# First block of a fused SSM and SwiGLU kernel: a row sent by another engine, one tile's statistics on another engine, an earlier copy, and buffers at other addresses

## The chip, the cores and the metric

The kernel runs on one core of a Trainium2 chip. The metric is the device time of one execution in microseconds (us). A core has five engines that run their own instruction queues in order and wait for one another by semaphores: TensorE (PE; its weight loads are shown apart as PEld), VectorE (DVE), ScalarE (ACT), GpSimd (POOL) and SyncE (SP). SyncE and ScalarE issue the DMAs of this kernel.

## The reference

2048 tokens of 448 channels pass through two branches, each with a layer norm that a small conditioning vector shifts, scales and gates.

```python
x = A_u
mod = (_silu(c) @ w_mod).reshape(c.shape[0], 6, 1, -1)
sa, ca, ga, sb, cb, gb = (mod[:, 0], mod[:, 1], mod[:, 2], mod[:, 3], mod[:, 4], mod[:, 5])
h = _layernorm(x, axis=-1) * (1 + ca) + sa
x = x + ga * _A_ref(h, ...)      # state-space convolution along the tokens
h = _layernorm(x, axis=-1) * (1 + cb) + sb
x = x + gb * _B_ref(h, ...)      # (silu(h @ w_gate) * (h @ w_up)) @ w_down, 1792 hidden
```

## The kernel before

**Tiles and blocks.** A tile is 128 tokens by 448 channels. The sixteen tiles form six blocks of 2, 2, 3, 3, 3 and 3. A prologue computes the modulation rows, a test flag and the first branch of tiles 0 and 1. Then `run_blocks` goes block by block: `ffn` does the second branch of the block, and between its matmuls the first branch of the next block's tiles is done.

**Slices.** In `ffn` the hidden width is cut into 14 slices of 128. Slice f has `gate_up(f)` (L750: 22 matmuls with the tokens' high and low parts `hhi` and `hlo` as moving operand and the weights `gu` as stationary one), then ScalarE's SiLU (L765), VectorE's product (L778), and the product's high part `phi` (ScalarE, L785) and low part `plo` (VectorE, L786). `down(f)` (L798) multiplies these with the down weights' parts `wdh` and `wdl`, and stands one slice later on TensorE. In block 0 the weights are still raw: ScalarE makes the high parts (L122, L123, L115) and VectorE the low ones (L125, L117) in the course of the slices.

**The first branch.** For each tile of the next block: mean and variance, normalised and modulated h, then cumulative sums over tokens by matmuls with a triangular matrix (L978, L979 in block 0), to which a row carried from the tile before is added (`run0`, `run1`; added at L946 and L947 by VectorE). The carried row is computed on partitions 96 to 127 (L987, L988) and one small DMA takes partition 127's row to partition 0. Then the second norm's statistics follow, and at the end of the block `make_xn` (L207 to L209) and eight or twelve transposes (L220) give the next block's `hhi` and `hlo`.

**Order.** It is written by hand. In the prologue the string `PLAN` is the order; `qtb` is the copy of the gate row's four partial rows into `gb` (ScalarE), `gbk` the matmul that adds them up and spreads them (L495), `gb` its copy back, `xn0` the scaling of tile 0's normalised rows (L510). In the blocks `TIMES` gives half-slices: h places a step after `gate_up(h // 2)`, ahead of the down product (h even) or behind it (h odd). In block 0 statistics come from `Norm.sums`: ScalarE adds up a copy of the tile, GpSimd divides by 448, ScalarE adds up the squares of the differences. In later blocks `Norm.stat` takes them on VectorE with two instructions.

```python
                    at(0, 1, lambda: sc.dma_start(run[0:1], run[127:128]))
...
                    elif not b:
                        go(h, n2.sums, nx[q], nx, 0)
                        go(h + 1, n2.sums, nx[q], nx, 1)
```

Of the kernel before, what the change touches and what calls it, by code (L numbers as in the profile page):

```python
# [8 lines left out]
F32 = mybir.dt.float32  # L9
# [3 lines left out]
OP = mybir.AluOpType  # L13
# [16 lines left out]


TIMES = (
# [3 lines left out]
)  # L36
# [4 lines left out]
ORDER = """sf x0 x1 sc m10 se sd m11 m20 m21 m00 sb m01 sa m40 m41 m30 m31 w0 w1 d0 m50 m51 d1 x2 w2 x3 d2"""  # L41

PLAN = """t4 pa0 t1 S1 t2 pa1 t3 wi ca gp S20 wr ps0 h00 gpc gt h01 S21 psx gac a2 sq1 ps1 m0 dg gdm t5 k0 gdr S3 h10 cp v00 dga a3 o00
m1 k1 cpc gd h11 hd0 ck v01 sq0 o10 v10 w0 cbw o12 v11 w01 o01 o02 hd1 o13 o14 xh1 gc0 sa d00 gc1 st0 r0 sp x1 st1 r1 n10 gq fs spc n11 xn0 sbt qtb sbc fl l1
gbk tr0 xn1 xn1b gb tr1 hi00 hi01 hi10 tr1b lo00 lo01 hi11 lo10 lo11 w1 w11 fr1 fx"""
EPS = 1e-5

# [9 lines left out]
def tile_kernel(ctx, tc, x, a_re, a_im, b_re, b_im, c_re, c_im, log_dt,  # L57
# [78 lines left out]
    g0 = const.tile([128, D], F32)  # L136
    gm0 = const.tile([128, D], F32)
    gm1 = g0
    hhi = const.tile([128, 4, MB * 128], F32R)
    hlo = const.tile([128, 4, MB * 128], F32R)  # L140
    gd = const.tile([128, D], F32)
    sbc = const.tile([128, 4], F32)
    flag = const.tile([1, 1], I32)
    half = const.tile([128, 1], F32)

    small = ctx.enter_context(tc.tile_pool(name="small", bufs=2))

# [5 lines left out]
    class Norm:  # L153
# [10 lines left out]
        def sums(self, i, ts, z):  # L164

            if i == ts[0] and not z:
                self.mv = small.tile([128, MB, 2], F32, name="mv" + self.tag)
            m, v = (self.mv[:, i - ts[0], k:k + 1] for k in range(2))
            if not z:
                sc.activation(h_of(i), xs[i], AF.Copy, accum_out=m)  # L170
                po.tensor_scalar(m, m, 1.0 / D, None, op0=OP.mult)
            else:
                sc.activation(h_of(i), xs[i], AF.Square, scale=-1.0, bias=m, accum_out=v)

        def root(self, ts, summed=False):
            rs = small.tile([128, MB], F32, name="rs" + self.tag)
            n = len(ts)
            if summed:
                po.tensor_scalar(rs[:, 0:n], self.mv[:, 0:n, 1], 1.0 / D, EPS, op0=OP.mult, op1=OP.add)
            else:  # L180
                po.tensor_scalar(rs[:, 0:n], self.mv[:, 0:n, 1], EPS, None, op0=OP.add)  # L181
            po.tensor_tensor(rs[:, 0:n], rs[:, 0:n], mhalf.to_broadcast([128, n]), op=OP.pow)
            for q, i in enumerate(ts):
                self.of[i] = self.mv[:, q, 0:1], rs[:, q:q + 1]
# [30 lines left out]
    def transposes(ts):  # L215
        n = len(ts) * 128
        for k in range(4):
            ps = CV if k == 2 else bank()
            for j, i in enumerate(ts):
                pe.transpose(ps[:, j * 128:(j + 1) * 128], xn[i][:, k * 128:(k + 1) * 128], ident)  # L220
            parts(hhi[:, k, 0:n], hlo[:, k, 0:n], ps[:, 0:n], k)

    xd = [dram.tile([128, 512], F32, name=f"xd{q}") for q in range(MB)]

# [9 lines left out]
    def split_turned(ts):  # L234
        n, m = len(ts) * 128, len(ts)
        for k in range(4):
            hi, lo = (h[:, k, 0:n].rearrange("p (q a r) -> p q a r", q=m, a=4) for h in (hhi, hlo))
            parts(hi, lo, turned[:, 0:m, :, k, :], k)

    wp0 = ctx.enter_context(tc.tile_pool(name="wp0", bufs=1))  # L240
    ones = const.tile([128, 1], F32)
    mhalf = const.tile([128, 1], F32)
    ntok = const.tile([128, 1], F32)
    cs = const.tile([128, 5], F32)
    pick = const.tile([128, 1], F32)
    gac = const.tile([128, 4], F32)

    def mod_part(ps, w, ks):
# [34 lines left out]
    with tc.tile_pool(name="pre", bufs=1) as pre:  # L283
# [153 lines left out]

        def high(q, ks=range(4)):
            for k in ks:
                c_ = slice(q * 128, (q + 1) * 128)  # L440
                sc.activation(hhi[:, k, c_], pk[q, k][:, k * 128:(k + 1) * 128], AF.Identity, bias=sbc[:, k:k + 1])

        def high_v(q, ks):
            for k in ks:
                c_ = slice(q * 128, (q + 1) * 128)
                ve.tensor_scalar(hhi[:, k, c_], pk[q, k][:, k * 128:(k + 1) * 128], sbc[:, k:k + 1], None, op0=OP.add)

        def low(q, ks=range(4)):
            for k in ks:
                c_ = slice(q * 128, (q + 1) * 128)  # L450
                ve.scalar_tensor_tensor(hlo[:, k, c_], pk[q, k][:, k * 128:(k + 1) * 128], sbc[:, k:k + 1], f32(hhi[:, k, c_]),
                                        op0=OP.add, op1=OP.subtract)

# [272 lines left out]
    def run_blocks(pools, stages, first=None):  # L726
        work, hid = pools.work, pools.hid
        def ffn(ts, fresh, last, todo):
# [4 lines left out]
            def gate_up(f, nw):  # L733
                head = fresh and f < 2
                if fresh and f:
                    split_d(f)
                w = wgu[f]
                p = hid.tile([128, 256], F32, name="p") if fresh else p_of[f % 2]
                hi = hid.tile([128, MB * 128], F32R, name="phi")
                lo = hid.tile([128, MB * 128], F32R, name="plo")  # L740
                ps = [bank(), bank()]

                top = [(k, a) for k, ws in enumerate(((0, 6), (1, 5), (2, 4), (3,))) for a in ws]
                low = [(k, k) for k in range(4)]

                def mm(s, ka, lo, first=False, end=False):
                    for q, (k, a) in enumerate(ka):
                        pe.matmul(ps[s][:, 0:n], w[:, s, a], (hlo if lo else hhi)[:, k, 0:n],  # L750
                                  start=first and q == 0, stop=end and q == len(ka) - 1)
# [24 lines left out]
                if nw is not None:  # L776
                    split_w(nw, 0)
                ve.tensor_tensor(ps[1][:, 0:n], p[:, 0:n], ps[1][:, 0:n], op=OP.mult)  # L778
                if fresh and f == 0:
                    split_d(0, 1)  # L780
                    for g, a in todo.get("mid", []):
                        g(*a)
                elif nw is not None:
                    split_w(nw, 1)
                sc.copy(hi[:, 0:n], ps[1][:, 0:n])  # L785
                ve.tensor_tensor(lo[:, 0:n], ps[1][:, 0:n], f32(hi[:, 0:n]), op=OP.subtract)  # L786
                if fresh and f == 0:
                    split_w(nw, 1)
# [86 lines left out]
        for b, ts in enumerate(TILES):  # L875
            todo = {}
            if b + 1 < len(TILES):
# [14 lines left out]
                if b == 0 and first is None:  # L892
                    go(EXTRA[0], gate_0)
                    todo["mid"] = [(first_rows, ())]
                    at(0, 1, lambda: sc.dma_start(run[0:1], run[127:128]))
                for i, h in zip(nx, stat1):
                    if b:
                        go(h, n1.stat, i, nx)
                    else:
                        go(h, n1.sums, i, nx, 0)  # L900
                        go(h + 1, n1.sums, i, nx, 1)
                go(root1, n1.root, nx, not b)

                for h, q, z in sorted((h, q, z) for q, hs in enumerate(times) for z, h in enumerate(hs)):
                    if z < len(times[q]) - 1:
                        if z < len(st):
                            go(h, st[z], nx[q])
                    elif not b:
                        go(h, n2.sums, nx[q], nx, 0)
                        go(h + 1, n2.sums, nx[q], nx, 1)  # L910
                    elif late:
# [4 lines left out]
                        go(h + 1, make_xn, nx[q], t_of[q])  # L916
                        go(h + 2, turn, nx[q], q)
                if late:
                    go(late[0], n2.root, nx, not b)
# [5 lines left out]
    def small_path(pools):  # L925
# [58 lines left out]
        def s5(i):  # L984
            o, s = vs.pop(i)
            if i + 1 < NT:
                sc.copy(run1[end], s[end])  # L987
                ve.scalar_tensor_tensor(run0[end], run1[end], 128.0, o[end], op0=OP.mult, op1=OP.add)  # L988
                sc.dma_start(run[0:1], run[127:128])
            ve.tensor_tensor(xs[i], xs[i], o, op=OP.add)  # L990
            ve.scalar_tensor_tensor(xs[i], s, tok, xs[i], op0=OP.mult, op1=OP.add)

# [108 lines left out]
```

## Time and profile before

| | |
|---|---|
| median of 3 runs | 485.16 us (485.07 to 485.28) |
| the profiled execution | 485.64 us, of which 483.8 us from the first to the last instruction |
| TensorE matmul busy | 471.3 us, 97% |
| VectorE, ScalarE, GpSimd busy | 282.6 us (58%), 161.2 us (33%), 60.4 us (12%) |
| granted TensorE clock | 1.0 throughout |
| prologue, block 0, block 1, rest | 0 to 34.0, to 95.4, to 152.8, to 483.8 us |

Times of rows are counted from the span's start. Matmuls are pipelined, so the length of a matmul's row overlaps with the next one's; from one start to the next is what it takes. In brackets behind a row of the timeline stands how long the engine was idle ahead of it and what ended that.

### The profile page before, as it was taken

The page shows a single profiled execution, that of the slowest core. Times are in us where ns is not written, and L with a number is a line of the kernel's source. Part 1 is how long each engine was busy: PE and PEld are TensorE (multiplying, and loading weights), DVE is VectorE, ACT ScalarE, POOL GpSimd, SP SyncE. Part 2 cuts the span into 40 slices and gives each one's busy share as a digit, 9 for nine tenths or more (in the row PEclk, how much of TensorE's full clock was granted, in tenths as well). Part 3 has the DMA queues.
Part 4 walks back from the last instruction along what each step waited for, and adds up shares of the span by engine and source line. Part 5 has one row for each costly group of instructions (what it writes and reads, how often), then busy time and mean ns, then how long its engine had stood idle before and what let it go on. Part 6 is the DMA issues. An engine that isn't in the chain of part 4 may idle for free.

```text
span 483.8 us, 7024 instructions
## 1 busy us (share of the span) xinstructions
PE 471.3 (97%) x2735; PEld 445.5 (92%) x2735; DVE 282.6 (58%) x538; ACT 161.2 (33%) x363; POOL 60.4 (12%) x86
## 2 busy tenths in 40 slices
PE   6999999799999999999999999999999999999995
PEld 4659999699999999999999999999999999999995
DVE  5878997768785546573644756375475544221225
ACT  5868656522234222332312323221223232112111
POOL 1221000000000040310022320002241000000000
PEclk9999999999999999999999999999999999999999
DMA  8955653030001100111200011130001112000001
GB/s 307 416 212 170 195 181 103 0 96 2 1 2 46 51 1 0 45 41 48 95 20 1 2 44 45 43 115 0 2 0 45 45 43 77 22 2 0 1 0 63
DMA packets 18779, 31.24 MB, mean 65 GB/s; under 512 B 2608, under 2 KB 13488, under 8 KB 18736
## 3 DMA queue, kind: packets, MB, share of 16 engines
q1 hardware_dynamic: 18000, 30.52, 18.6%
q8 instruction: 23, 0.38, 0.4%
q10 hardware_dynamic: 736, 0.19, 0.2%
q14 instruction: 20, 0.16, 0.1%
HBM read 24.61 MB, written 6.03 MB: 63 GB/s over the span
## 4 chain that ended last, share of the span: by engine, by line
PE 86%; DVE 6%; ACT 3%; DMA 3%; issue 1%; SPq 0%; POOL 0%; ACTq 0%; DVEq 0%
PE bank L750 56%; PE dn L798 25%; DMA wm<-in_w_mod_groups_dram 2%; DVE gu L125 1%; DMA vec<-in_c_log_dt_dram 1%; DVE plo L786 1%; DVE wdl L117 1%; PE bank L252 1%; PE cv L968 1%; PE cv L966 1%; PE bank L967 1%; ACT gu L122 0%; DVE bank L778 0%; DVE x L837 0%; PE bank L220 0%
## 5 line engine op out<-in xcount | busy, mean ns | idle before, releaser
L750 PE MATMUL bank<-hhi,gu 128*128 128x384 f32 (+1 forms) x1176 | 213.0, 320 | 0.2 <-issue 0.2
L750 PEld LDWEIGHTS bank<-hhi,gu 128*128 128x128 f32 x1176 | 192.7, 188 | 3.5 <-issue 1.1
L750 PE MATMUL bank<-hlo,gu 128*128 128x384 f32 (+1 forms) x672 | 133.2, 320 | 0.0
L750 PEld LDWEIGHTS bank<-hlo,gu 128*128 128x128 f32 x672 | 111.0, 188 | 0.2
L778 DVE TENSOR_TENSOR bank<-raw,bank 128x384 f32<-128x384 f32 (+1 forms) x69 | 36.9, 535 | 125.2 <-PE bank L750 122.7
L785 ACT CAST phi<-bank 128x384 fp32r<-128x384 f32 (+1 forms) x83 | 36.8, 443 | 137.7 <-DVE bank L778 137.6
L765 ACT ACTIVATE raw<-bank 128x384 f32<-128x384 f32 (+1 forms) x70 | 32.9, 470 | 124.2 <-PE bank L750 116.0
L786 DVE TENSOR_TENSOR plo<-bank,phi 128x384 fp32r<-128x384 f32 (+1 forms) x83 | 42.5, 512 | 37.1 <-ACT phi L785 37.1
L798 PE MATMUL dn<-wdh,phi 128*128 128x448 f32 x218 | 57.8, 367 | 1.0 <-ACT phi L785 1.0
L798 PE MATMUL dn<-wdh,plo 128*128 128x448 f32 x218 | 58.0, 367 | 0.3 <-DVE plo L786 0.3
L798 PE MATMUL dn<-wdl,phi 128*128 128x448 f32 x218 | 57.8, 366 | 0.0
L798 PEld LDWEIGHTS dn<-wdh,plo 128*128 128x128 f32 x218 | 40.8, 188 | 4.6 <-DVE plo L786 1.0
L798 PEld LDWEIGHTS dn<-wdl,phi 128*128 128x128 f32 x218 | 41.0, 188 | 3.2
L798 PEld LDWEIGHTS dn<-wdh,phi 128*128 128x128 f32 x218 | 38.8, 188 | 2.4 <-ACT phi L785 1.2
L181 POOL TENSOR_SCALAR rsb<-mvb 128x1 f32<-128x1 f32 (+1 forms) x12 | 4.2, 346 | 135.2 <-DVE mvb L151 135.2
L125 DVE TENSOR_TENSOR gu<-raw,gu 128x1024 fp32r<-128x1024 f32 x14 | 17.1, 1221 | 2.5 <-ACT gu L123 2.5
L181 POOL TENSOR_SCALAR rsa<-mva 128x3 f32<-128x3 f32 (+1 forms) x5 | 1.9, 388 | 101.4 <-DVE mva L151 101.4
L117 DVE TENSOR_TENSOR wdl<-rawd,wdh 128x448 fp32r<-128x448 f32 x16 | 9.9, 620 | 5.8 <-ACT wdh L115 5.7
L941 POOL TENSOR_TENSOR m<-m,gm 128x448 f32<-128x448 f32 x9 | 10.4, 1150 | 21.4 <-DVE m L198 17.6
L955 DVE TENSOR_TENSOR vl<-m,vh 128x448 fp32r<-128x448 f32 x12 | 9.1, 759 | 6.7 <-ACT vh L954 6.1
L122 ACT CAST gu<-raw 128x768 fp32r<-128x768 f32 x14 | 11.6, 830 | 0.0
L960 POOL TENSOR_TENSOR m<-m,gd 128x448 f32<-128x448 f32 x9 | 11.5, 1279 | 0.0
(245 smaller groups left out, 407.2 us busy)
## 6 DMA issues: line engine op xcount, KB each, us to landing
raw<-in_B_w_gate_up_dram SPq DMA_DIRECT2D x14, 512.0 KB, 3.8
rawd<-in_B_w_down_dram SPq DMA_DIRECT2D x16, 224.0 KB, 3.9
x<-in_A_u_dram SPq DMA_DIRECT2D x12, 224.0 KB, 3.2
out_dram<-x SPq DMA_DIRECT2D x11, 224.0 KB, 1.9
xd<-raw SPq DMA_DIRECT2D x9, 256.0 KB, 2.1
raw<-xd SPq DMA_DIRECT2D x36, 64.0 KB, 1.9
wm<-in_w_mod_groups_dram SPq DMA_DIRECT2D x5, 448.0 KB, 8.0
wm<-in_w_mod_groups_dram SPq DMA_DIRECT2D x5, 336.0 KB, 8.0
```

The costliest lines, as they stand in the source:

```text
L117: ve.tensor_tensor(lo, wdn[j], f32(hi), op=OP.subtract)
L122: sc.copy(wgu[j][:, :, 0:3, :], w[:, :, 0:3, :])
L125: ve.tensor_tensor(wgu[j][:, :, 3:7, :], w[:, :, ::-1, :], f32(wgu[j][:, :, 0:4, :][:, :, ::-1, :]), op=OP.subtract)
L750: pe.matmul(ps[s][:, 0:n], w[:, s, a], (hlo if lo else hhi)[:, k, 0:n], start=first and q == 0, stop=end and q == len(ka) - 1)
L765: sc.activation(p[:, 0:n], ps[0][:, 0:n], AF.Silu)
L778: ve.tensor_tensor(ps[1][:, 0:n], p[:, 0:n], ps[1][:, 0:n], op=OP.mult)
L785: sc.copy(hi[:, 0:n], ps[1][:, 0:n])
L786: ve.tensor_tensor(lo[:, 0:n], ps[1][:, 0:n], f32(hi[:, 0:n]), op=OP.subtract)
L798: pe.matmul(dn[q][:, 0:D], u[:, cs], v, start=f == 0 and z == 0, stop=f == (NF - 3 if last else NF - 1) and z == 2)
L941: (ve if on_v else po).tensor_tensor(v, h, g, op=OP.mult)
L955: ve.tensor_tensor(vl, v0, f32(vh), op=OP.subtract)
L960: (ve if on_v else po).tensor_tensor(h, h, gd, op=OP.mult)
```

## The change

1. **Rows sent by SyncE.** The small DMA of the carried row in block 0 (three of them: at the block's beginning, and after tiles 2 and 3) is issued by SyncE in place of ScalarE.
2. **Last tile's statistics on VectorE.** The second norm's statistics of tile 3 are taken by `Norm.stat` (VectorE), as in later blocks. Those of tile 2, and the first norm's of both, stay on ScalarE and GpSimd; there the division is folded into the Square's scale, for which GpSimd writes the scaled mean into a further column of `cs`. In `TIMES`, tile 3's first statistics and the root behind them come a half-slice later, and the second norm's root a half-slice sooner.
3. **The gate row's parts copied sooner.** `qtb` moves ahead of `n11 xn0` in `PLAN`.
4. **Other addresses.** Small constants move ahead of `hhi` in the constants' pool, and `mhalf` and `half` become one tile. In the built program `hhi` and `hlo` start 128 bytes further up, and what the later pools hold (weights, their parts, `phi`, `plo`) 32 bytes further down. In blocks of two tiles the parts stand in columns 48 to 303 in place of 0 to 255.

```diff
-    ((1, 2), 4, ((5, 10, 13, 15, 15, 16), (9, 9, 17, 19, 20, 20)), 21, (22, 23)),
+    ((1, 3), 5, ((5, 10, 13, 15, 15, 16), (9, 9, 17, 19, 20, 20)), 20, (22, 23)),
...
-m1 k1 cpc gd ... n10 gq fs spc n11 xn0 sbt qtb sbc fl l1
+m1 k1 cpc gd ... n10 gq fs spc qtb n11 xn0 sbt sbc fl l1
...
+    ones = const.tile([128, 1], F32)
+    halves = const.tile([128, 2], F32)
+    mhalf, half = halves[:, 0:1], halves[:, 1:2]
+    ntok = const.tile([128, 1], F32)
+    pick = const.tile([128, 1], F32)
+
+    first_col = lambda n: 48 if n == 256 else 0
     hhi = const.tile([128, 4, MB * 128], F32R)
     hlo = const.tile([128, 4, MB * 128], F32R)
...
                 sc.activation(h_of(i), xs[i], AF.Copy, accum_out=m)
+                po.tensor_scalar(cs[:, 5:6], m, D ** -1.5, None, op0=OP.mult)
                 po.tensor_scalar(m, m, 1.0 / D, None, op0=OP.mult)
             else:
-                sc.activation(h_of(i), xs[i], AF.Square, scale=-1.0, bias=m, accum_out=v)
+                sc.activation(h_of(i), xs[i], AF.Square, scale=-(D ** -0.5), bias=cs[:, 5:6], accum_out=v)
...
-                        pe.matmul(ps[s][:, 0:n], w[:, s, a], (hlo if lo else hhi)[:, k, 0:n],
+                        pe.matmul(ps[s][:, 0:n], w[:, s, a], (hlo if lo else hhi)[:, k, first_col(n):first_col(n) + n],
...
-                    at(0, 1, lambda: sc.dma_start(run[0:1], run[127:128]))
+                    at(0, 1, lambda: sy.dma_start(run[0:1], run[127:128]))
...
-                    elif not b:
+                    elif not b and not q:
                         go(h, n2.sums, nx[q], nx, 0)
                         go(h + 1, n2.sums, nx[q], nx, 1)
...
-                sc.dma_start(run[0:1], run[127:128])
+                (sy if i in TILES[1] else sc).dma_start(run[0:1], run[127:128])
```

How the instructions stand on ScalarE at the end of the prologue, before (`qts` are the shift row's parts, `h_0` and `h_1` the normalised rows of tiles 0 and 1):

```order
L488 COPY qts<-bank 128x448
L510 ACTIVATE h_0_252<-h_0_252,rsb 128x448
L473 COPY gb<-bank 128x448
L511 ACTIVATE h_1_253<-h_1_253,rsb 128x256
L441 ACTIVATE hhi<-bank,sbc 128x128 x4
```

and after the change:

```order
L489 COPY qts<-bank 128x448
L474 COPY gb<-bank 128x448
L511 ACTIVATE h_0_251<-h_0_251,rsb 128x448
L512 ACTIVATE h_1_252<-h_1_252,rsb 128x256
L442 ACTIVATE hhi<-bank,sbc 128x128 x4
```

The copy into `gb` has moved ahead of the scaling of tile 0.

ScalarE in slices 10 and 11 of block 0, before (the first row is `phi` of slice 10, the last that of slice 11; `x_75` is tile 3):

```order
L785 CAST phi<-bank 128x256
L987 COPY run<-bank 32x448
L989 DMA run<-run 1x16x56
L170 ACTIVATE m_79,mvb<-x_75 128x448
L173 ACTIVATE m_79,mvb<-x_75,mvb 128x448
L115 CAST wdh_916<-rawd_83 128x448
L765 ACTIVATE p<-bank 128x256
L122 CAST gu_914<-raw 128x2x384
L123 ACTIVATE gu_914<-raw,half 128x2x128
L785 CAST phi<-bank 128x256
```

and after the change:

```order
L786 CAST phi<-bank 128x256
L988 COPY run<-bank 32x448
L115 CAST wdh_917<-rawd_83 128x448
L766 ACTIVATE p<-bank 128x256
L122 CAST gu_915<-raw 128x2x384
L123 ACTIVATE gu_915<-raw,halves 128x2x128
L786 CAST phi<-bank 128x256
```

The DMA and the two sums over tile 3 are gone from ScalarE.

VectorE at the same place, after the change (from the carried row of tile 3 to the low parts of slice 11; before, the two BN rows are not there and all else stands alike):

```order
L989 SCALAR_TENSOR_TENSOR run<-run,cv 32x448
L991 TENSOR_TENSOR x_75<-x_75,cv 128x448
L992 SCALAR_TENSOR_TENSOR x_75<-bank,tok,x_75 128x448
L156 BN_STATS stb<-x_75 128x6
L157 BN_AGGR mvb<-stb 128x2
L117 TENSOR_TENSOR wdl_918<-rawd_83,wdh_917 128x448
L779 TENSOR_TENSOR bank<-p,bank 128x256
L125 TENSOR_TENSOR gu_915<-raw,gu_915 128x2x512
L787 TENSOR_TENSOR plo<-bank,phi 128x256
```

The statistics stand ahead of slice 11's work. On SyncE the three row DMAs stand in the queue of weight loads: the first behind the loads of slice 0, the second behind those of slice 7, the third behind all of block 0's. TensorE's order is the same as before.

More of the change, by code (lines that the diff above doesn't have):

```diff
@@ L43 @@
 PLAN = """t4 pa0 t1 S1 t2 pa1 t3 wi ca gp S20 wr ps0 h00 gpc gt h01 S21 psx gac a2 sq1 ps1 m0 dg gdm t5 k0 gdr S3 h10 cp v00 dga a3 o00
-m1 k1 cpc gd h11 hd0 ck v01 sq0 o10 v10 w0 cbw o12 v11 w01 o01 o02 hd1 o13 o14 xh1 gc0 sa d00 gc1 st0 r0 sp x1 st1 r1 n10 gq fs spc n11 xn0 sbt qtb sbc fl l1
+m1 k1 cpc gd h11 hd0 ck v01 sq0 o10 v10 w0 cbw o12 v11 w01 o01 o02 hd1 o13 o14 xh1 gc0 sa d00 gc1 st0 r0 sp x1 st1 r1 n10 gq fs spc qtb n11 xn0 sbt sbc fl l1
 gbk tr0 xn1 xn1b gb tr1 hi00 hi01 hi10 tr1b lo00 lo01 hi11 lo10 lo11 w1 w11 fr1 fx"""
@@ L143, in tile_kernel @@
     flag = const.tile([1, 1], I32)
-    half = const.tile([128, 1], F32)
     small = ctx.enter_context(tc.tile_pool(name="small", bufs=2))
@@ L170, in sums, with root @@
                 sc.activation(h_of(i), xs[i], AF.Copy, accum_out=m)
+                po.tensor_scalar(cs[:, 5:6], m, D ** -1.5, None, op0=OP.mult)
                 po.tensor_scalar(m, m, 1.0 / D, None, op0=OP.mult)
             else:
-                sc.activation(h_of(i), xs[i], AF.Square, scale=-1.0, bias=m, accum_out=v)
-        def root(self, ts, summed=False):
+                sc.activation(h_of(i), xs[i], AF.Square, scale=-(D ** -0.5), bias=cs[:, 5:6], accum_out=v)
+        def root(self, ts):
             rs = small.tile([128, MB], F32, name="rs" + self.tag)
             n = len(ts)
[L178 to L181, printed above, removed]
+            po.tensor_scalar(rs[:, 0:n], self.mv[:, 0:n, 1], EPS, None, op0=OP.add)
             po.tensor_tensor(rs[:, 0:n], rs[:, 0:n], mhalf.to_broadcast([128, n]), op=OP.pow)
@@ L220, in transposes @@
                 pe.transpose(ps[:, j * 128:(j + 1) * 128], xn[i][:, k * 128:(k + 1) * 128], ident)
-            parts(hhi[:, k, 0:n], hlo[:, k, 0:n], ps[:, 0:n], k)
+            c_ = slice(first_col(n), first_col(n) + n)
+            parts(hhi[:, k, c_], hlo[:, k, c_], ps[:, 0:n], k)
     xd = [dram.tile([128, 512], F32, name=f"xd{q}") for q in range(MB)]
@@ L236, in split_turned @@
         for k in range(4):
-            hi, lo = (h[:, k, 0:n].rearrange("p (q a r) -> p q a r", q=m, a=4) for h in (hhi, hlo))
+            hi, lo = (h[:, k, first_col(n):first_col(n) + n].rearrange("p (q a r) -> p q a r", q=m, a=4) for h in (hhi, hlo))
             parts(hi, lo, turned[:, 0:m, :, k, :], k)
     wp0 = ctx.enter_context(tc.tile_pool(name="wp0", bufs=1))
[L241 to L245, printed above, removed]
+    cs = const.tile([128, 6], F32)
     gac = const.tile([128, 4], F32)
@@ L439, in high @@
             for k in ks:
-                c_ = slice(q * 128, (q + 1) * 128)
+                c_ = slice(48 + q * 128, 176 + q * 128)
                 sc.activation(hhi[:, k, c_], pk[q, k][:, k * 128:(k + 1) * 128], AF.Identity, bias=sbc[:, k:k + 1])
@@ L444, in high_v @@
             for k in ks:
-                c_ = slice(q * 128, (q + 1) * 128)
+                c_ = slice(48 + q * 128, 176 + q * 128)
                 ve.tensor_scalar(hhi[:, k, c_], pk[q, k][:, k * 128:(k + 1) * 128], sbc[:, k:k + 1], None, op0=OP.add)
@@ L449, in low @@
             for k in ks:
-                c_ = slice(q * 128, (q + 1) * 128)
+                c_ = slice(48 + q * 128, 176 + q * 128)
                 ve.scalar_tensor_tensor(hlo[:, k, c_], pk[q, k][:, k * 128:(k + 1) * 128], sbc[:, k:k + 1], f32(hhi[:, k, c_]),
@@ L901, in run_blocks @@
                         go(h + 1, n1.sums, i, nx, 1)
-                go(root1, n1.root, nx, not b)
+                go(root1, n1.root, nx)
                 for h, q, z in sorted((h, q, z) for q, hs in enumerate(times) for z, h in enumerate(hs)):
@@ L918, in run_blocks @@
                 if late:
-                    go(late[0], n2.root, nx, not b)
+                    go(late[0], n2.root, nx)
                     for q, (h, i) in enumerate(zip(late[1], nx)):
```

## The prediction

> **What bounds the kernel now.** I read the page first, for the busy engines, then the windows of the program's stages, then who waited for whom on TensorE's weight loads, and last the timeline where those waits stand.
>
> ```profile
> span 483.8 us, 7024 instructions
> PE 471.3 (97%) x2735; PEld 445.5 (92%) x2735; DVE 282.6 (58%) x538; ACT 161.2 (33%) x363; POOL 60.4 (12%) x86
> ```
>
> TensorE is the bound: only what lets it start sooner or wait less can show. The windows (stretch, its length, then busy time of PE, PEld, DVE, ACT, POOL, the granted clock, DMA) say where it waits:
>
> ```profile
> 28.00:34.01 6.01, 4.98 (x42) 2.71 (x34) 4.01 (x12) 3.02 (x8) 1.47 (x4) 1.00 0.37 116
> 34.01:82.18 48.17, 48.02 (x337) 45.32 (x337) 44.19 (x79) 32.47 (x76) 2.21 (x5) 1.00 0.53 170
> 82.18:95.41 13.23, 10.76 (x71) 9.50 (x70) 7.82 (x16) 9.00 (x23) 1.14 (x3) 1.00 0.00 0
> 95.41:152.81 57.40, 57.40 (x415) 55.90 (x414) 43.75 (x89) 18.32 (x44) 2.24 (x4) 1.00 0.07 21
> ```
>
> The first row is the end of the prologue, the second slices 0 to 11 of block 0, the third its last two slices and the turn into block 1, the fourth block 1. PE has holes in the first and the third and none in the fourth. The granted clock is 1.00 in all, so clock is no term here. The weight loads between 25 and 100 us (line and what it waited for, us in total, times, longest) name the holes:
>
> ```profile
> PEld bank L220 <- DVE plo L786: 1.4, 1, 1.4
> PEld bank L495 <- ACT gb L473: 1.2, 1, 1.2
> PEld dn L798 <- ACT phi L785: 1.2, 1, 1.2
> PEld dn L798 <- DVE plo L786: 1.0, 2, 0.6
> PEld bank L978 <- DVE v L947: 0.5, 1, 0.5
> ```
>
> L495 is in the prologue; of the others, all but L978 and one 0.4 us wait of L798 are in the third window.
>
> **The gate row (prologue).** Start, length, engine, line:
>
> ```profile
> 28.41 0.54 PE L265 MATMUL bank<-m,cs 128*32 128x224 f32 x2
> 30.12 0.67 ACT L510 ACTIVATE h<-h,rsb 128x448 f32<-128x448 f32 x1 [1.46 <-DVE h L455]
> 30.69 0.51 ACT L473 COPY gb<-bank 128x448 f32<-128x448 f32 x1
> 31.26 1.02 PE L495 MATMUL bank<-gb,pick 128*128 128x448 f32 x2 [0.85 <-ACT gb L473]
> ```
>
> The source of the copy into gb is finished at 28.95 (28.41 + 0.54), yet the copy stands behind xn0 (L510), which waits 1.46 us for VectorE. Moved ahead of xn0 it runs at about 29.0 to 29.5, inside that 1.46 us, so xn0 still starts at 30.12. L495 then starts when TensorE is free, 0.85 us sooner. What is late next? The transposes behind it need xn0, ready at 30.79, and would now start near 31.26: 0.5 us of room. **Term: -0.85 us.**
>
> **ScalarE loses the row's DMA and a stall (slices 0 to 11).**
>
> ```profile
> 39.81 0.58 ACT L170 ACTIVATE m<-x 128x448 f32<-128x448 f32 x1 [1.14 <-issue]
> 44.16 0.67 ACT L173 ACTIVATE m<-x,mva 128x448 f32<-128x448 f32 x1 [0.32 <-POOL mva L171]
> 68.58 0.57 ACT L115 CAST wdh<-rawd 128x448 fp32r<-128x448 f32 x1 [2.93 <-DVE run L988]
> DVE gu L125 <- ACT gu L123: 1.7, 4, 0.5
> DVE wdl L117 <- ACT wdh L115: 1.5, 1, 1.5
> ```
>
> The 1.14 us is the row's first DMA issued from ScalarE (ACTq L895); the 2.93 us is ScalarE held until VectorE had written the row that the second DMA sends. Both leave. The second square of block 0's statistics (0.67 and 0.32 of waiting) goes behind slice 2's own work. So wdh of slice 2 comes about 2 us sooner. The last two rows are VectorE's waits between 40 and 78 us: 3.2 us, all for ScalarE's weight parts. TensorE does not see them as such, but VectorE runs almost without a gap (44.19 of 48.17 us busy) and ends this stretch late, so what it no longer waits it is ahead. I let it be ahead by up to 3.2 us less what it has to wait for TensorE. The two small waits of TensorE (0.5 at L978, 0.4 at L798) go with that. At L495 the load waited 1.2 and the matmul 0.85, and at the L798 that waits for phi 1.2 and 0.96 (shown below), so some 0.25 of each is load time that hid anyway: 0.9 - 0.5 = 0.4. **Term: -0.4 us.**
>
> The folding of the scale into Square changes no length on ScalarE. GpSimd gets one more small operation per tile (I take 0.2 to 0.7 us), behind the one that ScalarE waits for; nothing waits for it but the root. No cost.
>
> **The end of block 0.**
>
> ```profile
> 77.08 0.56 PE L798 MATMUL dn<-wdh,phi 128*128 128x448 f32 x2
> 77.93 0.42 DVE L778 TENSOR_TENSOR bank<-p,bank 128x256 f32<-128x256 f32 x1
> 81.16 0.68 DVE L991 SCALAR_TENSOR_TENSOR x<-bank,tok,x 128x448 f32<-128x448 f32 x1
> 81.87 0.58 ACT L170 ACTIVATE m<-x 128x448 f32<-128x448 f32 x1 [2.56 <-DVE x L991]
> 85.94 0.68 PE L798 MATMUL dn<-wdh,phi 128*128 128x448 f32 x2 [0.96 <-ACT phi L785]
> 87.13 1.27 DVE L207 SCALAR_TENSOR_TENSOR raw<-x,mvb,cbw 128x448 f32<-128x448 f32 x2
> 92.27 0.44 PE L220 MATMUL bank<-ident,raw 128*128 128x128 f32 x2 [1.14 <-DVE plo L786]
> 100.85 1.23 PE dn L798 x6
> 102.09 2.64 PE bank L750 x22
> 149.07 0.66 PE bank L220 x6
> 150.38 2.43 PE dn L798 x12
> ```
>
> The last four rows are the chain of waits in block 1, which has the same widths and no holes: 1.23 a down slice, 2.64 a gate slice, 0.11 a transpose, 2.43 two downs. Without holes the third window is 2.64 + 1.23 + 2.64 + 8 x 0.11 + 2.43 = 9.82; it took 13.23, so 3.41 is lost. The cause: ScalarE sits 2.56 us until VectorE has finished tile 3's x, then does both sums, and only then the casts and SiLU of slice 11, so phi comes late for TensorE at 85.94, and everything to 92.27 after it.
>
> After the change slice 11 on ScalarE waits for TensorE alone. VectorE carries tile 3's statistics; the same pair in the prologue:
>
> ```profile
> 28.61 0.63 DVE L150 BATCH_NORM_STATS2 stb<-x 128x6 f32<-128x448 f32 x1
> 29.27 0.18 DVE L151 BATCH_NORM_AGGREGATE mvb<-stb 128x2 f32<-128x6 f32 x1
> 63.74 0.60 DVE L117 TENSOR_TENSOR wdl<-rawd,wdh 128x448 fp32r<-128x448 f32 x1
> 66.08 0.60 DVE L960 TENSOR_TENSOR m<-m,gd 128x448 f32<-128x448 f32 x1
> ```
>
> VectorE's string from slice 10's product to the transposes: 77.93 to the end of L991 at 81.84 is 3.91; the pair 0.63 + 0.18 + 0.05 of gaps is 0.86; slice 11's four operations without a wait are 2.34 (63.74 to 66.08); from L207 to TensorE's L220 it is 92.27 - 87.13 = 5.14. Sum 12.25. TensorE from the end of slice 10 (77.08) to the same transposes needs 3 x 1.23 + 3 x 2.64 + 0.22 = 11.83. If VectorE starts the string 0.05 after slice 10 ends, TensorE still waits 12.30 - 11.83 = 0.47 us there. In the old profile VectorE starts it 0.85 late; TensorE itself will be 1.25 earlier, so VectorE has to be 2.05 us earlier than it was, against 3.2 us of waits that can go. **Term: -(3.41 - 0.47) = -2.94 us.**
>
> **The row's DMA on SyncE.**
>
> ```profile
> 66.22 0.43 SPq L110 DMA_DIRECT2D rawd<-in_B_w_down_dram  x1
> rawd<-in_B_w_down_dram SPq DMA_DIRECT2D x16, 224.0 KB, 3.9
> run<-run ACTq DMA_DIRECT2D x14, 3.5 KB, 1.7
> 72.19 0.60 DVE L946 TENSOR_TENSOR m<-m,run 1x448 f32<-1x448 f32 x1
> ```
>
> On SyncE it waits for VectorE's row behind loads already issued, the last at 66.22, landing about 70.1 (3.9 later). Issued at 68.0, it would land at 69.7 alone and at most 1.7 after that load, 71.8, if it is served last. Its reader stands at 72.19, or 71.7 with the 0.47 us of the table's wait before it gone. Cost between 0 and 0.1; I take 0. Behind it on SyncE stand only loads of weights for later slices, and the third one stands ahead of the blocks' output alone. [...]
>
> **The addresses.** In the built program hhi and hlo lie 128 bytes higher, two-tile slices 192 more, and weights, phi and plo 32 lower. No row shows such a shift. The nearest is the gate slice: 22 matmuls take 2.64 us at 256 columns (120 ns) and in the three-tile blocks
>
> ```profile
> 162.44 3.89 PE bank L750 x22
> ```
>
> 177 ns at 384: 0.44 ns a column. Upper bound: 32 bytes are 8 columns; were each matmul to fetch 8 more, 3.5 ns on 2,600 matmuls, +9 us. Lower bound: of 120 ns only 7 are not proportional to columns; half a ns of it on 2,600 is -1.3 us. I take 0, since weights of every slice lie elsewhere and their slices cost the same. [...]
>
> **Sum.** -0.85 - 0.4 - 2.94 = -4.2 us. Against the profiled execution, 485.64 us (483.8 of span), that is 481.4; its time is 0.48 above the median of 485.16, so 481.0.
>
> **Rivals.** *VectorE does not come forward* (its row arrives late over SyncE, or the string is bound by itself): then slice 10's product stays at 77.93 and the transposes come at 77.93 + 12.25 = 90.18 instead of 92.27, -2.1 in all, 483.1. For it: VectorE is busy 92% of that stretch; against: 3.2 us of its waits have their cause removed. *The prologue gives nothing*, because something else than gb holds the first transposes: 481.8. Against it: every other input is there 0.5 us ahead. *The new addresses slow TensorE*: slower than before from 4.2 / 2,600 = 1.6 ns a matmul on; at the bound of 3.5 ns 485.2 - 4.2 + 9.1 = 490. For it: the weight loads are 92% busy, so there is little slack to hide a slower one; against: equal slices at all addresses so far. *They quicken it*: 479.7. *It does nothing that counts* (ScalarE's removed waits return as waits for VectorE's products, and gb's copy still comes after xn0): 485.2.
>
> **Chances.** Forecast 0.60; VectorE not forward 0.15; prologue 0.08; addresses slower 0.08; addresses quicker 0.06; nothing 0.03. The range 479.4 to 483.3 holds the forecast with an error of its tail term, both smaller gains and the quicker addresses; it leaves out the slower addresses and no change. A change of 0.2% (1 us) is about what can be told from none: faster 0.89, same 0.03, slower 0.08.
>
> **What would show it.** Right: no wait of L495 for gb; no wait of ScalarE's wdh cast for run; L798 without a wait for phi in slice 11; one wait of about 0.5 us left at the block's transposes; 22 matmuls of a gate slice still 2.64 and 3.89. Wrong: VectorE waiting at its row additions for a DMA; transposes still more than 1 us late; or a gate slice of another length.

## The result, and the profile after

The changed kernel takes 477.07 us (median of 6, 476.9 to 478.23), the kernel before on the same chip 485.25 us (485.07 to 486.28): ratio 0.9835, 95% interval 0.9821 to 0.9849. By the ratio it is faster by 8.0 us where 4.2 were forecast; 477.07 lies 2.3 us below the low end of the range. Its profiled execution took 478.08 us, 475.9 of it span.

The page of the changed kernel, first the span and then each engine's busy time:

```profile
span 475.9 us, 7026 instructions
PE 465.3 (98%) x2735; PEld 439.4 (92%) x2735; DVE 282.8 (59%) x540; ACT 160.2 (34%) x359; POOL 62.4 (13%) x88
```

The other engines are about as busy as before (GpSimd 2.0 us more, ScalarE 1.0 less). TensorE is busy for 465.3 us where it was 471.3, with the same 2735 matmuls. Such a drop inside the matmuls is the first sign of a term that the forecast lacks. Not all 6 us belong to it: the kernel with the new schedule alone (below) is busy for 469.4 us, so the schedule accounts for 1.9 and the addresses for the other 4.1.

The windows of the same four stages (end of the prologue, slices 0 to 11 of block 0, its last two slices and the turn, block 1):

```profile
28.00:33.34 5.34, 5.16 (x41) 2.79 (x36) 4.05 (x12) 3.22 (x8) 1.52 (x4) 1.00 0.38 119
33.34:79.47 46.13, 46.13 (x336) 43.90 (x337) 44.02 (x79) 34.31 (x79) 4.19 (x8) 1.00 0.56 181
79.47:90.87 11.40, 10.10 (x71) 9.27 (x70) 8.43 (x19) 6.00 (x15) 1.19 (x2) 1.00 0.00 0
90.87:147.30 56.43, 56.35 (x415) 54.61 (x414) 43.49 (x89) 18.31 (x44) 2.23 (x4) 1.00 0.07 22
```

Against before the first row lost 0.67, the second 2.04, the third 1.83, the fourth 0.97, and the 328.6 us behind them 2.4. From block 1 on no instruction has moved, and block 1 had no hole; by the forecast these stretches should have stayed.

What the weight loads waited for between 25 and 100 us (line, us in total, times, longest), and the two places of the timeline on which the forecast rested:

```profile
PEld bank L224 <- DVE plo L787: 1.4, 1, 1.4
...
PEld bank L224 <- ACT p L766: 0.4, 1, 0.4
```

```profile
30.70 0.92 PE L496 MATMUL bank<-gb,pick 128*128 128x448 f32 x2
...
87.73 0.44 PE L224 MATMUL bank<-ident,raw 128*128 128x128 f32 x2 [1.15 <-DVE plo L787]
```

The gate row's matmul (L496, before L495) waits for nothing now, and the waits of the down products for phi and plo are gone. Among the matmuls of this stretch one such wait is left, at the transposes (L224), but of 1.15 us, where 0.47 was forecast.

The chain of waits, in block 1 and in a block of three tiles, shows where the rest is:

```profile
101.19 2.51 PE bank L751 x22
103.69 1.23 PE dn L799 x6
...
440.31 3.82 PE bank L751 x22
444.13 1.85 PE dn L799 x9
```

A gate slice takes 2.51 where it took 2.64, and 3.82 where it took 3.88 or 3.89. The prediction named "a gate slice of another length" as what would make it wrong.

### The profile page after: what moved, and what is told of

Read it like the earlier page. It is cut to its first block, busy times and chain, and to the rows that moved or that the text cites. A ratio compares the mean times of both kernels' runs of the same rounds, so it can differ in the third digit from the quotient of the medians.

```text
span 475.9 us, 7026 instructions
## 1 busy us (share of the span) xinstructions
PE 465.3 (98%) x2735; PEld 439.4 (92%) x2735; DVE 282.8 (59%) x540; ACT 160.2 (34%) x359; POOL 62.4 (13%) x88
## 4 chain that ended last, share of the span: by engine, by line
PE 89%; DVE 4%; DMA 3%; ACT 2%; issue 1%; SPq 0%; DVEq 0%; ACTq 0%
PE bank L751 56%; PE dn L799 27%; DMA wm<-in_w_mod_groups_dram 2%; DMA vec<-in_c_log_dt_dram 1%; ACT raw L213 1%; PE dn L473 1%; DVE bank L779 1%; PE bank L253 1%; PE bank L968 0%; PE cv L967 0%; PE cv L969 0%; DVE plo L787 0%; PE bank L263 0%; SPq L297 0%; ACT phi L786 0%
## 5 line engine op out<-in xcount | busy, mean ns | idle before, releaser
L751 PE MATMUL bank<-hhi,gu 128*128 128x384 f32 (+1 forms) x1176 | 209.2, 317 | 0.2 <-issue 0.2
L751 PEld LDWEIGHTS bank<-hhi,gu 128*128 128x128 f32 x1176 | 189.8, 188 | 3.8 <-issue 1.1
L751 PE MATMUL bank<-hlo,gu 128*128 128x384 f32 (+1 forms) x672 | 130.6, 316 | 0.0
L751 PEld LDWEIGHTS bank<-hlo,gu 128*128 128x128 f32 x672 | 109.1, 188 | 0.2
L766 ACT ACTIVATE raw<-bank 128x384 f32<-128x384 f32 (+1 forms) x70 | 32.8, 469 | 123.0 <-PE bank L751 114.1
L185 POOL TENSOR_SCALAR rsb<-mvb 128x1 f32<-128x1 f32 (+2 forms) x13 | 4.6, 354 | 143.8 <-DVE mvb L157 143.8
```

## The experiments

"Pace" is the mean time from one matmul's start to the next one's, over all pairs of neighbours of one line and shape, worked out from the records of a trace; the few intervals of over 250 ns at 256 columns are left out. "Distance" is the start of the moving operand less that of the stationary one, modulo 256 bytes, in the built program: parts less `gu` for the gate slices, down weights less `phi` for the down products.

### The schedule and the addresses apart

The first kernel has parts 1 to 3 of the change and the addresses of before. Against the changed kernel:

```diff
-    first_col = lambda n: 48 if n == 256 else 0
+    first_col = lambda n: 0
```

with the small constants back in their old places. The second has the addresses alone.

> Parts 1 to 3 of the change with every address as before. Theory A (the new addresses shorten TensorE's matmuls, the schedule gives what was forecast): 22 gate matmuls still 2.64 us at 256 columns and 3.88 at 384, and 481.0 us in all, 4.2 less than before, with one wait of some 0.5 us left at the block's transposes. Theory B (the matmuls are shorter because the other engines now do something else beside them): gate slices 2.51 and 3.82, about 477.5 us.

> Part 4 alone, the order of instructions as before. Theory A: gate slices 2.51 and 3.82 us as after the change; blocks 1 to 5 give 3.4 us (57.40 to 56.5 and 322.0 to 319.5), block 0 next to nothing, since its end waits for ScalarE and VectorE: about 481.7 us. Theory B: gate slices 2.64 and 3.88, 485.2 us.

Measured: schedule alone 481.29 us (480.77 to 481.64), ratio 0.9914 (0.9895 to 0.9934); addresses alone 481.69 us (481.64 to 482.6), ratio 0.9928 (0.9908 to 0.9948). By the ratios the two give 4.2 and 3.5 us, together 7.7 of the 8.0. The schedule's part is the forecast's 4.2. At the transposes of the schedule-only kernel (timeline, VectorE's product of slice 10 and TensorE):

```profile
75.52 0.43 DVE L778 TENSOR_TENSOR bank<-p,bank 128x256 f32<-128x256 f32 x1 [0.16 <-PE bank L750]
...
87.69 0.44 PE L219 MATMUL bank<-ident,raw 128*128 128x128 f32 x2 [0.47 <-DVE plo L786]
```

The wait is 0.47, as forecast, and VectorE's string from 75.52 to 87.69 is 12.17 where 12.25 was worked out. That it agrees to the hundredth is luck. Slice 10 ended at 75.25, so the string began 0.27 behind it and not 0.05, and TensorE took 11.97 to the transposes and not 11.83; these and the shorter string cancel.

The windows of this kernel (slices 0 to 11 of block 0, then the last two and the turn):

```profile
32.85:80.34 47.49, 47.49 (x336) 45.48 (x337) 44.97 (x82) 34.49 (x79) 4.20 (x8) 1.00 0.57 176
80.34:90.84 10.50, 10.03 (x72) 9.52 (x71) 7.61 (x16) 6.00 (x15) 1.20 (x2) 1.00 0.00 0
```

In the kernel with both parts VectorE's string stands at the same place, from 75.56 to 87.73:

```profile
75.56 0.42 DVE L779 TENSOR_TENSOR bank<-p,bank 128x256 f32<-128x256 f32 x1
```

Its product has no wait for TensorE any more: VectorE is the bound at the end of block 0. Both kernels begin block 1 at the same time, 90.84 and 90.87. What the shorter matmuls give in block 0 comes back as the wait of 1.15; the addresses' gain shows only from block 1 on. In the addresses-only kernel block 0 takes 61.40 us (33.78 to 95.18), just as before (34.01 to 95.41). That kernel has the new lengths (chain of waits):

```profile
101.58 2.51 PE bank L753 x22
104.09 1.23 PE dn L801 x6
...
444.45 3.82 PE bank L753 x22
```

### Two parts of the schedule by themselves

The first has only the three row DMAs on SyncE, the second only tile 3's statistics on VectorE (with the folded scale); `TIMES` and `PLAN` are those of before in both.

```diff
-                    at(0, 1, lambda: sc.dma_start(run[0:1], run[127:128]))
+                    at(0, 1, lambda: sy.dma_start(run[0:1], run[127:128]))
...
-                sc.dma_start(run[0:1], run[127:128])
+                (sy if i in TILES[1] else sc).dma_start(run[0:1], run[127:128])
```

```diff
-                    elif not b:
+                    elif not b and not q:
```

> Part 1 alone: the carried row's three DMAs from SyncE, all else as before. If ScalarE's waits for the row delay VectorE's string, the stretch up to slice 12 gets rid of the small waits and VectorE is about 1.5 us ahead at slice 10, but tile 3's sums stay on ScalarE behind VectorE's x: half of the end's loss stays, about 483.5 us. If the row then comes late, the row additions on VectorE wait for a DMA and nothing is won: 485.3 us.

> Part 2 alone, with the old half-slices: tile 3's second statistics on VectorE. ScalarE still issues the row's DMA behind VectorE's row (until about 81.0) but not the sums: slice 11's cast comes at 81.0 in place of 83.5. About 2 us of the end's 3.4 are won, 483.3 us; if VectorE's string is the bound even so, with 0.8 us more in it, 484.5 us.

Measured, one execution each, beside 485.12 of before: the row 485.88 us, the statistics 482.95. With the row alone the end of block 0 keeps its waits (timeline):

```profile
84.69 0.67 PE L798 MATMUL dn<-wdh,phi 128*128 128x448 f32 x2 [0.91 <-ACT phi L785]
86.02 0.67 PE L798 MATMUL dn<-wdh,plo 128*128 128x448 f32 x2 [0.25 <-DVE plo L786]
91.02 0.44 PE L220 MATMUL bank<-ident,raw 128*128 128x128 f32 x2 [1.14 <-DVE plo L786]
```

The waits of the third window stand as they stood. That misses the expectation, by which half of the end's loss would go (483.5 us): VectorE's product of slice 10 does come 1.25 sooner (76.68 for 77.93), but ScalarE's sums still stand in the way. What the row gives lies ahead of the end, in slices 0 to 11:

```profile
33.39:80.99 47.60, 47.60 (x337) 45.39 (x337) 44.02 (x79) 32.60 (x76) 2.66 (x5) 1.00 0.54 173
```

They took 48.17 before and take 48.19 in the statistics-only kernel (33.56 to 81.75), so the row's move is worth 0.57 there. Block 1 began 1.26 us sooner, of which 0.62 was there at slice 0 already, ahead of any moved row. The execution still ended no sooner. The last row of its chain of waits, and the one of before:

```profile
476.30 1.74 DVE x L837 x4
```

```profile
477.59 1.74 DVE x L837 x4
```

VectorE's last additions come 1.29 us sooner, at a span of 483.9 against 483.8: what stands behind them, the transfer out, was 1.4 us longer in this execution. One execution doesn't tell why. With the statistics alone phi's wait is gone and the transposes wait 1.04:

```profile
89.67 0.44 PE L218 MATMUL bank<-ident,raw 128*128 128x128 f32 x2 [1.04 <-DVE plo L784]
```

From slice 12 to block 1 it is 11.06 us (81.75 to 92.81) where it was 13.23. So the statistics' move makes 2.2 of the tail term; with the other moves VectorE comes forward, and 1.04 goes down to 0.47.

### One address at a time

Against the kernel before: the parts of two-tile blocks in columns 48 to 303 (192 bytes up), at all places that write or read them; all pools behind `hhi` 32 bytes lower (`half` and `mhalf` in one tile); `hhi`, `hlo` and `gd` 128 bytes higher and the rest where it was (four small constants ahead of `hhi`).

```diff
+    first_col = lambda n: 48 if n == 256 else 0
```

```diff
-    half = const.tile([128, 1], F32)
+    halves = const.tile([128, 2], F32)
+    mhalf, half = halves[:, 0:1], halves[:, 1:2]
...
-    mhalf = const.tile([128, 1], F32)
```

```diff
+    ones = const.tile([128, 1], F32)
+    mhalf = const.tile([128, 1], F32)
+    ntok = const.tile([128, 1], F32)
+    pick = const.tile([128, 1], F32)
     hhi = const.tile([128, 4, MB * 128], F32R)
...
```

> Only the tokens' parts of two-tile blocks stand in columns 48 to 303, 192 bytes further up; weights, phi, plo and the base of hhi as before. If the place of the moving operand alone decides, 256-column gate slices fall from 2.64 to about 2.51 us and 384-column ones stay at 3.88; some 484 us. If it is the place of the weights, all stays: 485.2 us.

> Only the later pools (weights and their parts, phi, plo) lie 32 bytes lower; hhi and its columns as before. If the place of the stationary operand decides, 384-column gate slices fall from 3.88 to 3.82 us, 256-column ones from 2.64 to 2.51, and a three-tile down slice goes from 1.835 to 1.85: about 482 us. If the moving operand decides, gate slices stay and only the down slices, whose both operands moved, get longer: some 486 us.

> Only hhi and hlo (and gd behind them) start 128 bytes further up; the columns and all later pools as before. If moving and stationary operand act each by itself, 384-column gate slices take 3.83 us (the 3.81 of the new addresses less the 0.02 that the lower weights gave) and 256-column ones lie between 2.58 and 2.64; about 483 us. If only both together act, 3.88 and 485.3 us.

Measured: column 48 484.71 us (484.06 to 485.85), ratio 0.9974 (0.9956 to 0.9992); weights lower 484.28 (483.69 to 485.38), ratio 0.9973 (0.9961 to 0.9986); parts higher 481.2, one execution beside 485.12. Each moves another pace: column 48 only that of 256 columns (120.3 to 117.2 ns), weights lower both a little (119.1, and 176.5 to 175.9), parts higher that of 384 columns most (173.9). In the chain of waits, a gate slice of each kernel in this order:

```profile
102.00 2.57 PE bank L752 x22
...
441.60 3.89 PE bank L752 x22
```

```profile
101.78 2.62 PE bank L750 x22
...
440.81 3.88 PE bank L750 x22
```

```profile
102.16 2.60 PE bank L750 x22
...
444.18 3.83 PE bank L750 x22
```

None of the three times was hit: the gate slices of the first two lie between what either theory gave, and for the third, whose slices came as expected (3.83, and 2.60 between 2.58 and 2.64), 483 was too high a sum: 1232 x 2.6 ns at 384 columns is 3.2 us alone. Nor do the gains add up. At 384 columns the weights give 0.6 ns and the parts 2.6, together they give 2.7 to 2.8; at 256 columns 3.1 + 1.2 + 1.5 is 5.8, and together they give 4.6 to 4.8 (there two of the three move the same operand, so that sum tests less). Two places that act each by itself do not explain this; a relation between them might.

### All distances, TensorE by itself

Two kernels leave the computation out and run gate slices back to back: the first with the parts' and the weights' starts stepped by 32 bytes each, the second with the distance in steps of 16 and down products behind each gate slice at eight distances of their own.

```diff
+    for s, q, k, a in G: pe.matmul(ps[s][:, 0:256], w(32, s, a), m(256, 40, k), start=q == 0, stop=q == 10)
+    for s, q, k, a in G: pe.matmul(ps[s][:, 0:256], w(32, s, a), m(256, 48, k), start=q == 0, stop=q == 10)
...
```

> None of the computation is done: TensorE alone, every other engine idle, runs groups of 22 matmuls in the order of a gate slice (256 columns, then 384), each group with moving and stationary operand at other byte addresses modulo 512, in steps of 32. If the addresses alone set the length, the group with moving at 416 and stationary at 320 (as before the change) takes 2.64 us, moving 96 and stationary 320 about 2.58, moving 416 and stationary 288 about 2.62, moving 224 and stationary 288 (as after) about 2.54, and at 384 columns 3.88 for moving 416 with stationary 320 and 3.81 for moving 32 with stationary 288. If what the other engines read and write beside TensorE sets it, all groups of a width are alike, within 0.02 us.

> The whole computation is left out; the output is zeros. TensorE runs 256 slices back to back with nothing to wait for: 128 three-tile slices (22 matmuls of 384 columns, then 9 down products of 448) and 128 two-tile slices (22 of 256, then 6 of 448). The start of the parts against the weights, modulo 256 bytes, goes through 0 to 240 in steps of 16; that of the down weights against phi through 0, -32, ... -224. Theory (a matmul's pace is set by how far the moving operand's start lies from the stationary one's, modulo 256 bytes): the 22 take the same at each phi, 173 to 177 ns at 384 columns and 113 to 120 at 256, slowest at 0 and 96 for 256 columns and at 96 to 128 for 384; the down products, too, depend on their own difference alone, and in the changed kernel's case (difference 0) they take the same 203 to 204 ns whatever the parts' place is. Rival (the pace also depends on what ran just before, so that a slice comes into one of several rhythms and keeps it): the down products at difference 0 take 203.9 ns behind parts at 96 and 205.6 behind parts at 0, as in the kernels before and after, and 256 columns at 192 take 113.3 in some slices and 117.8 in others. A step of 16 bytes between two places of 32 gives a value between theirs by the theory of distance; by a theory of 32-byte units it gives that of one of its neighbours.

In the first, 256 columns, the chain of waits (each line of the kernel is one pair of places; a and c are the two halves of a slice):

```profile
44.43 1.29 PE c L73 x11
45.72 1.30 PE a L74 x11
47.02 1.30 PE c L74 x11
48.33 1.31 PE a L75 x11
49.64 1.32 PE c L75 x11
```

L73, L74 and L75 have the same weights, and parts 32 bytes apart (distances 192, 224 and 0): the 11 matmuls take 1.29, 1.30 and 1.32 in the half c. Over all pairs of places (32 a distance at 256 columns, 6 at 384) the pace goes by the distance, nearly wherever the two operands lie: at 384 columns distance 64 gives 173.4 to 173.5 in all six and 96 gives 176.4 to 176.6, while the six spread by 0.7 to 2.1 ns at 0, 192 and 224; at 256 columns the pairs of one distance lie within 0.7 ns at 0, 64, 96, 128 and 224. They spread more at 32 (116.6 to 118.1), 160 (117.3 to 120.0) and 192 (114.1 to 118.0).

The second gives the same curve with more points. ns a matmul, median over the eight down distances:

| distance | 0 | 32 | 64 | 96 | 112 | 128 | 160 | 192 | 224 | 240 |
|---|---|---|---|---|---|---|---|---|---|---|
| 256 columns | 119.6 | 117.0 | 117.8 | 119.8 | 115.3 | 118.6 | 118.5 | 114.7 | 118.2 | 117.2 |
| 384 columns | 174.5 | 176.6 | 173.5 | 176.5 | 173.6 | 175.8 | 173.8 | 174.1 | 173.6 | 179.4 |
| down, three tiles | 202.8 | 204.9 | 200.8 | 205.2 | | 203.6 | 202.2 | 202.4 | 204.2 | |

112 lies below both 96 and 128: steps of 16 bytes count. The slowest place of 384 columns, 240, is one that steps of 32 had not touched; 96 to 128 had been expected. At 384 columns distance 32 differs between the two kernels: 173.3 in all of the first, mostly 176.6 in the second, where down products run in between. The down products settle the second question. At distance 64 all 16 groups of three-tile slices lie between 200.0 and 201.4; at distance 0 ten lie at 202 to 203 and five at 206 to 208, by the place of the parts in the gate slices around them, which is all that differs among them. The chain, three groups at distance 0 and then three at 64:

```profile
43.69 1.82 PE dn L71 x9
...
49.36 1.86 PE dn L71 x9
...
55.03 1.82 PE dn L71 x9
```

```profile
589.36 1.81 PE dn L71 x9
...
595.01 1.80 PE dn L71 x9
...
600.63 1.80 PE dn L71 x9
```

So both theories hold a part: the distance sets the pace, and at some distances there are two rhythms (two paces at the same addresses), of which the stretch ahead picks one. That is how the changed kernel's down products (203.8 to 205.6 ns on the mean, 203 to 207 in the median) could grow longer at an unchanged distance.

### The places put where the grid is quickest, and all places moved together

The first two kernels are the changed one with `phi` and `plo` 192 bytes up (first cut below); in the first of them the parts move as well (second cut, with the matching columns where the parts are written). The third is the kernel before with everything from `hhi` on 96 bytes higher (third cut).

```diff
+            gap.tile([128, 48], F32, name="gap")
             self.hid = es.enter_context(tc.tile_pool(name="hid", bufs=2))
```

```diff
-    first_col = lambda n: 48 if n == 256 else 0
+    sbc = const.tile([128, 4], F32)
+    flag = const.tile([1, 1], I32)
...
+    first_col = lambda n: 32 if n == 256 else 0
     hhi = const.tile([128, 4, MB * 128], F32R)
...
```

```diff
+    gap = const.tile([128, 24], F32)
     hhi = const.tile([128, 4, MB * 128], F32R)
```

> The kernel after the change, with the parts and phi put where the slice grid was quickest: parts 64 bytes above the weights modulo 256 in three-tile blocks, 192 in two-tile ones (sbc and flag stand ahead of hhi, the parts of two-tile blocks start in column 32), and phi and plo 192 bytes further up, so that the down weights lie 64 above them modulo 256. By the theory that the pace is set by the distances, with the grid's own prices: 173.3 ns at 384 columns (173.8 before), 200.8 a down product in three-tile blocks (205.6 before), about 114.5 at 256 columns (115.5) and 201.5 a down product in two-tile blocks (204.2). Three-tile blocks: 56 x (22 x 0.5 + 9 x 4.8) ns = 3.0 us; block 1: 14 x (22 x 1.0 + 6 x 2.7) = 0.5; block 0 gives nothing, VectorE's string sets its end: 473.5 us. Rival (in the whole kernel other engines' reads and writes decide the down products' length, not the place): 205 ns as now, 476 to 477. [...]

> The kernel after the change, with phi and plo alone 192 bytes further up: the down weights then lie 64 above them modulo 256, where it was 0. By the theory of distances the gate slices stay at 173.8 and 115.5 ns a matmul and the down products go from 205.6 to 200.8 (three tiles) and from 204.2 to 201.5 (two): 56 x 9 x 4.8 + 14 x 6 x 2.7 ns = 2.6 us, 474.4 us. By the theory that the down products' length is set by the rhythm that the parts' place leaves, or by other engines: 205, and 477.

> The kernel before the change, with an unused 96 bytes ahead of hhi: parts, weights, phi and plo all lie 96 bytes further up, and no distance among them changes. By the theory of distances all stays as it was: 120.3 ns at 256 columns, 176.5 at 384, 203.8 a down product, 485.2 us. By a theory of places as such (lines of 32, 64, 128 or 256 bytes that an operand's start may cut) at least one of the three changes by over 1 ns: hhi goes from 160 to 0 modulo 256, the weights from 64 to 160.

Measured: best places **474.07 us** (473.24 to 474.42), ratio to before 0.9769 (0.9747 to 0.9791); phi alone 475.69 (474.74 to 475.9), ratio 0.9795 (0.9771 to 0.9819); all higher 485.11 in one execution, beside 485.18. The chain of waits of the three, in that order:

```profile
103.91 2.51 PE bank L752 x22
106.42 1.20 PE dn L800 x6
...
155.40 3.81 PE bank L752 x22
159.21 1.81 PE dn L800 x9
```

```profile
156.18 3.84 PE bank L751 x22
160.02 1.80 PE dn L799 x9
```

```profile
101.80 2.64 PE bank L751 x22
104.44 1.24 PE dn L799 x6
```

The paces beside their distances, for all kernels:

| kernel | 256 columns | 384 columns | down, three tiles |
|---|---|---|---|
| before; schedule only; all higher | 96: 120.3 | 96: 176.5 | 0: 203.8 |
| column 48 only | 32: 117.2 | 96: 176.5 | 0: 203.8 |
| weights lower only | 128: 119.1 | 128: 175.9 | 0: 203.1 |
| parts higher only | 224: 118.8 | 224: 173.9 | 0: 202.9 |
| after | 192: 115.5 | 0: 173.8 | 0: 205.6 |
| phi alone | 192: 115.0 | 0: 174.5 | 64: 199.8 |
| best places | 192: 114.9 | 64: 173.4 | 64: 200.5 |

Moving everything together changes no pace; what counts is the distance. The kernel at the best places is 3.0 us below the changed one, where 3.5 were worked out. Phi alone missed its 474.4 by 1.3, mostly because the gate slices at distance 0 went from 173.8 to 174.5 (1232 x 0.7 ns = 0.9 us): that distance, too, has two rhythms in the grid, 173.5 and 174.5. The granted clock was 0.998 and 1.0 in the two, where the changed kernel's execution had 0.997: a lower clock has no part in this.

## Why the prediction was right on the schedule and wrong in its sum

- **Gate row, -0.85.** The wait is gone. Slice 0 begins at 33.34, and at 32.85 in the schedule-only kernel, against 34.01: -0.67 and -1.16. Kernels without this part began it between 33.39 and 34.17, so one execution can't size the term closer than to some 0.4 us. On the mean, eight traces without it begin at 33.80 and four with it at 32.99: -0.81, near the term.
- **Small waits, -0.4.** Slices 0 to 11 took 48.17 before and 47.49 in the schedule-only kernel (32.85 to 80.34): -0.68. The row-only kernel has -0.57 of it, so the cause named, ScalarE rid of the row's DMA, holds.
- **End of block 0, -2.94.** The last two slices and the turn took 13.23 before and 10.50 (80.34 to 90.84): -2.73, with the wait of 0.47 and the string within 0.1 us of what was worked out. In the changed kernel it is -1.83, since TensorE comes to the same VectorE sooner.
- **Row by SyncE, 0.** No cost shows: in the row-only kernel VectorE waits between 36 and 97 us for ScalarE's results alone (8.4 us in all) and for no DMA. What the move gives is in the small waits above.
- **"The addresses ... I take 0".** This step failed, and nearly all that the sum was off, 3.5 of 3.8 us by the addresses-only kernel, lies in it. Its reason was that "weights of every slice lie elsewhere and their slices cost the same". But tiles of `gu`, 7168 bytes, and of the down weights, 1792, are whole multiples of 256: every slice had the same distance (96 at the gate slices, 0 at the down products), and equal slices were no evidence on a distance of 192 or 0. The lower bound, half a ns on 2,600 matmuls, was too tight as well: the pace fell by 4.8 ns at 256 columns and 2.7 at 384, and rose by 1.8 for the down products. From block 1 on that is 14 x 22 x 4.8 + 56 x (22 x 2.7 - 9 x 1.8) ns = 3.9 us. From the schedule-only kernel's trace to the changed one's the stretch is 3.15 shorter: the gate slices give 4.7 (in block 1 by itself 4.1 ns a matmul), the down products take back 0.9, and the turn of block 1 and what stands behind the last matmul took some 0.3 more each in the changed kernel's execution. The rival "they quicken it" was the true case, priced at 1.3.
- All these shifts are multiples of 16 bytes. In the second grid kernel, whose steps are of 16, such shifts change the pace of 256 columns between 114.7 and 119.8 ns.

## What to carry to other kernels

Rows that agree are evidence only over what differs among them: before an address change is priced at nothing, look whether all rows share the very offset that it moves. Where matmuls stream back to back, as here, the distance of the moving from the stationary operand, modulo 256 bytes, is a setting worth a small grid: in the grid here the pace of 256 columns went from 114.7 to 119.8 ns with it, and in the kernel a pad of 192 bytes, two constants moved and another column offset gave 3.0 us more. And where two engines are close to even, as TensorE and VectorE were at the end of block 0 (11.97 and 12.17 us to the same transposes in the schedule-only kernel), expect what one gains to come back as a wait for the other; here that wait went from 0.47 to 1.15 us. Count such a gain only in the stretches where the other has room.

## What the runs showed of the hardware

- The pace of back-to-back matmuls depends on the distance of the two operands modulo 256 bytes: in the second grid kernel 114.7 to 119.8 ns at 256 columns, 173.5 to 179.4 at 384, 200.8 to 205.2 at 448. A period of 128 does not fit: at 384 columns distance 96 gives 176.5, and 224 gives 173.6. In the first grid kernel, whose starts go through 512 bytes, the pairs of places of one distance modulo 256 lie within 0.7 ns at five of the eight distances (256 columns); at 192 they spread most, from 114.1 to 118.0.
- Why the distance matters is not shown. Nor is told apart whether it is the distance to the weights in use or to those being loaded, since here all weights share one offset and the loads run beside the matmuls (439.4 us of loads and 465.3 of matmuls in the changed kernel's span of 475.9).
- At some distances there are two rhythms, kept through a stretch and picked by what ran ahead: 114 or 118 ns (256 columns, 192), 173.5 or 174.5 (384, 0), 203 or 207 (448, 0). In the second grid kernel only the slices around differ where the pace differs, so they pick it; how they do is open.
